# Gated mix of two attentions: how a step's scores and the last output sums are placed at the end of an output block

## The chip, the cores and the metric

The kernel runs on one core of one Trainium2 chip. The metric is the device time of one execution in microseconds (us). A core has TensorE (PE, the matmuls; PEld is its weight load), VectorE (DVE), ScalarE (ACT), GpSimd (POOL) and SyncE (SP, which issues most DMAs). Matmul results land in PSUM, eight banks of 128 x 512 fp32, which TensorE writes and ScalarE and VectorE read.

## The reference

```python
x = A_x                                   # 1 x 2048 x 512
g = sigmoid((x * gate_w).sum(-1, keepdims=True))
# branch A: 32 heads of 16, each position looks at 8 positions, 2 apart, behind it
attn = softmax(where(mask, einsum("bhsd,bhswd->bhsw", q, kg) * scale, -1e9))
a = einsum("bhsw,bhswd->bhsd", attn, vg)... @ wo_A
# branch B: 32 query heads of 16, one key and value head, over all 2048 positions
p = softmax(einsum("bhqd,bkd->bhqk", q, k) * scale)
b = einsum("bhqk,bkd->bhqd", p, v)... @ wo_B
return g * a + (1 - g) * b
```

## The kernel before

**Phases.** A front phase projects queries, keys and values and writes parts of them to DRAM scratch. The main phase (from line 1225) does branch B in 512 steps s = 16 u + kt. A unit u is one block of 512 queries and four heads (32 units), kt is one of 16 blocks of 128 keys. GpSimd works through branch A meanwhile. A short tail writes the last four row blocks of the output.

**One step.** The program is written out in the order in which each engine runs its instructions, by a planner in the kernel itself: `clk` holds its clocks of TensorE, ScalarE and VectorE, and `free` the time at which each PSUM bank comes free, from the constants of line 45. `exp_pair(s, pr)` (line 460) computes the scores of two of the four heads as two matmuls side by side (L465) into a pair of banks, e0 for pr = 0 and e1 for pr = 1 (`eb`), and ScalarE exponentiates the 128 x 1024 scores (L471). `weighted(s)` (line 477) multiplies the four exponentials by the values into the bank `po` (L480). In a usual step the order (line 1243) is `(0, "m2", "m1", 1)`: first scores of s, a pair of maxima in the two banks `m2`, perhaps a single in `m1`, second scores of s, and then `weighted(s - 1)`.

**Maxima.** The exponentials need each row's maximum before its unit begins. It is found by separate score matmuls, "halves" of 128 x 512 (L322), of which there are 2048, with a maximum over each on VectorE: `fill_pair` does two halves side by side in `m2` (tile pm, L344), `fill_one` does one in `m1` (tile ps, L356). `fill_ready(key, slack)` (line 856) gives one out if its bank is free within `slack` of the planner's TensorE clock. `singles(s)` (line 845) spreads over the steps left whatever the pairs, one a step, and the out blocks to come won't cover, so that it is used up by step 488. After that the place of `m2` is used by the tail's first products.

**Out blocks.** At steps 272, 400 and 448, the first of a unit each, `out_phase` (line 768) multiplies four row blocks j of the outputs of both branches by their weights (L780), the last four being left to the tail. The conditions of line 1248 choose the steps. Row x of the four sums in `eb[x % 2]`, so the last one (x = 3) in e1, in 24 items of two matmuls side by side. At item 5 of a row, `turn` (line 641) transposes branch A's part of this row into the other pair of banks (L645), from where ScalarE reads it twice (L651, L652); in the last row that is e0. At the row's end `out_store` (line 674) has ScalarE copy both banks to the tile `two` (L678), GpSimd add the two halves (L681) and SyncE store the sum (L682).

`stream` (line 722) runs the items and fills around them. For the block's length `m2` is given up and its two banks serve as `pd0` and `pd1` for differences: `fill_diff` (line 395) computes a difference of two halves (L393), which ScalarE rectifies (L405), and `fill_sum` (line 413) adds one half to it and takes the maximum of both on VectorE (L417) in `ps` or `po`. These are given out by tests on the planner's clocks in `side_fill` (line 687); `closing` stops new differences in the last items. `weighted(s - 1)` runs in the block's first row. `done` (line 783) is called after each item. Afterwards the banks are `m2` again, and step s goes on with its order.

Of the kernel before, what the change touches and what calls it, by code (L numbers as in the profile page):

```python
# [8 lines left out]
AF = mybir.ActivationFunctionType  # L9
# [32 lines left out]
LEAD, M2S, M1S, MARGIN = 1.5, 0.5, 0.3, 0.12  # L42


T_R, T_LAT, T_EXP, T_RED2, T_RED1, T_W, T_TTR = 0.235, 0.20, 0.92, 1.14, 0.61, 1.21, 0.74
# [3 lines left out]
def gated_mix_kernel(ctx, tc, xt, wa, wk, wq, wo_a, wo_b, out):  # L49
    nc = tc.nc  # L50
# [22 lines left out]
    pp2, m2 = None, None  # L73
# [4 lines left out]
    eb = []  # L78
# [5 lines left out]
    clk = {"pe": 0.0, "act": 0.0, "dve": 0.0}  # L84

    def after(eng, ready, dur):
        clk[eng] = max(clk[eng], ready) + dur
        return clk[eng]
# [188 lines left out]
    def place(v):  # L277
        return v if v <= NB else (v - NB - 1) % (NB - 2)

    def gone(v):  # L280
        return v - NB - 1 if v < 2 * NB - 1 else v - NB + 2
# [16 lines left out]
    free = {"m1": 0.0, "e0": 0.0, "e1": 0.0, "po": 0.0, "d0": 24.0, "d1": 24.0}  # L298
    tasks, shifted = [], set()
    hooks, pool, done = [], 0.0, set()  # L300
# [3 lines left out]
    def mark(inst, end, up=None):  # L304
        marks.append((ups[0] if up is None else up, end, inst.ins.name))

    def fillable():
        return bool(half) or bool(slots) and slots[0][0] < len(stacked) and stacked[slots[0][0]] <= clk["pe"]
# [148 lines left out]

    pe, pexp, exped, homes, turns = [], {}, {}, [], [0]

    def exp_pair(s, pr):  # L460
        bank, key = eb[pr], f"e{pr}"
        u, kt = divmod(s, NJ)
        for odd in range(2):
            b = 64 * odd
            nc.tensor.matmul(bank[:, odd, :], kst[b:b + 64, kt * P:(kt + 1) * P], qst[place(u)][b:b + 64, pr, :], start=True, stop=True)  # L465
        if len(homes) < 6:
            homes.append(px.tile([P, 2, 512], F32, name="pexp", bufs=6))
        k, y = divmod(turns[0] + 1, 2)
        turns[0] += 1
        e = homes[len(homes) - 1 if turns[0] < 6 else (2 * (k % 3) + (y ^ k // 3 % 2) - 1) % 6]  # L470
        got = nc.scalar.activation(e, bank, AF.Exp, scale=SCALE)  # L471
        free[key] = after("act", after("pe", free[key], T_R) + T_LAT, T_EXP)
        mark(got, free[key])
        exped[s] = free[key]
        pexp[s, pr] = e
# [156 lines left out]
    def prepare(j, n):  # L632
        nonlocal pool
        hi, lo = turned[j, 1] = [qst[NB - 2][:, x].rearrange("p (c q) -> p c q", c=C) for x in range(2)]
        own = ob[j // 4][:, :n, j % 4 * P:(j % 4 + 1) * P]
        nc.scalar.activation(hi[:, :n], own, AF.Copy)
        at = after("act", clk["pe"], 0.6)
        nc.gpsimd.tensor_sub(lo[:, :n], own, hi[:, :n].bitcast(F32))
        pool = max(pool, 1e3 * at) + 1300
# [25 lines left out]
    def out_items(j, n):  # L665
        items = []
        for k, m in ((1, n), (0, C)):
            for x, w in ((0, woh), (0, wol), (1, woh)):
                items += [(lambda c=c, x=x, k=k: turned[j, k][x][:, c, :], w[k][:, c, :]) for c in range(m)]
        return items  # L670

    parts, spare = {}, []

    def out_store(j, k):
        nonlocal pool
        del turned[j, 0], turned[j, 1]
        two = p2b[0].tile([P, 2, D], F32, name="two", bufs=2)
        nc.scalar.activation(two, eb[k], AF.Copy)  # L678
        free[f"e{k}"] = after("act", clk["pe"] + T_LAT, 0.92)
        pool = max(pool, 1e3 * clk["act"]) + 1300  # L680
        nc.gpsimd.tensor_add(two[:, 0], two[:, 0], two[:, 1])  # L681
        nc.sync.dma_start(out[0].rearrange("(p j) d -> p j d", j=NJ)[:, j, :], two[:, 0])  # L682

# [84 lines left out]
    def out_phase(js, n, s):  # L768

        m = 3 * (C + n)  # L770
        items = {}

        def mm(b, at):
            x, j, i = at
            if j not in items:
                items[j] = out_items(j, n)
                clk["pe"] = max(clk["pe"], free[f"e{x % 2}"])
            st, mv = items[j][i]
            h = slice(64 * b, 64 * b + 64)
            nc.tensor.matmul(eb[x % 2][:, b, :], st()[h], mv[h], start=(i == 0), stop=(i == m - 1))  # L780
            return T_R

        def done(at):
            x, j, i = at
            if i % 4 == 3:
                run_tasks()
                run_pool()
            if i == (5 if x else 1):
                turn(j, 1 - x % 2)
            if i == (8 if x else 6):  # L790
                later.pop(j)()
            if i == 3 * n and j != js[-1]:
                prepare(js[x + 1], n)
            if i == m - 1:
                out_store(j, x % 2)

        stream([(x, j, i) for x, j in enumerate(js) for i in range(m)], mm, done, s)

# [57 lines left out]
    def fill_ready(key, slack):  # L856
        if fillable() and free[key] <= clk["pe"] + slack:
            clk["pe"] = max(clk["pe"], free[key])
            if key == "m1":
                fill_one()  # L860
            elif half and (not slots or half[0][0] < slots[0][0] or slots[0][0] >= len(stacked)):
                fill_one(m2[:, 0, :], "m2")
            elif slots:
                fill_pair(m2, "m2")
            return True
# [34 lines left out]
    def run_tasks():  # L900
        for task in [t for t in tasks if t[0] <= clk["pe"]]:
            tasks.remove(task)
            task[1](*task[2])
# [113 lines left out]
    def run_pool():  # L1017
        nonlocal pool
        now = clk["pe"] * 1e3
        for h in sorted(hooks, key=lambda h: h[0]):  # L1020
            if h[0] <= now:
                hooks.remove(h)
                h[1](h[2])
                done.add(h[3])
        while pieces and pool < now + 2500:
            if blocked and not blocked[0]():
                break
            blocked.clear()
            x = next(pieces[0], None)
            if x is None:  # L1030
                pieces.clear()
            elif callable(x):
                blocked.append(x)
            else:
                pool = max(pool, now) + x
# [188 lines left out]
        del held[b][1:], read_d[b][1:]  # L1224
    phase2()
    pe.append(tc.alloc_tile_pool(name="weighted", bufs=1, side="right"))
    outs, due = 0, []
    for s in range(NS + 1):
        u, kt = divmod(s, NJ)
        if len(stacked) < NU and s >= 16 * (gone(len(stacked)) + 1):  # L1230
            stack(len(stacked))
        if s < NS and kt == 0 and u not in shifted:
            while u not in shifted:
                clk["pe"] += 0.5
                run_tasks()
                if u not in shifted and left.get(u, 1):
                    assert pause(4)
        v = min(x[0][0] for x in (half, slots, [(NU,)]) if x)
        need = left.get(v, NF // NU)
        steps = 16 * v - 6 - s  # L1240
        short = need - 2.8 * max(0, steps) if v < NU else 0
        lead = (NF - to_go()) / 64 - s / 16
        order = (0, "m2", "m1", 1) if s > 1 else (1, "m2", "m1", 0) if s else ()
        k, n = outs // 4, C - (outs >= NJ - 4)
        if outs == NJ - 4:
            if short > 0 and steps < 2:
                pause(short)
        elif due or outs < NJ and outs // NH in done and kt == 15 and NHG * (k + 1) - 1 in shaped and (lead < LEAD or s >= 16 * (NHG * (k + 2) + 1) - 1):
            if not due:
                prepare(outs, n)  # L1250
                due.append(n)
            else:
                out_phase(list(range(outs, outs + 4)), due.pop(), s)
                outs += 4
        elif short > 0 and steps < 2:
            pause(short)

        for which in order:
            if which == "m2":
                if slots or half:  # L1260
                    fill_ready("m2", M2S)
                else:
                    next(tail, None)
            elif which == "m1":
                if singles(s) and fill_ready("m1", M1S):
                    owing[0] -= 1.0
            elif s < NS:
                exp_pair(s, which)
        if s - 1 in exped:
            weighted(s - 1)  # L1270
            if kt == 0 and s < NS:
                finish_a(u - 1, nc.gpsimd)
        run_tasks()
        run_pool()
# [14 lines left out]
    for x in range(2):  # L1289
        js = slice(2 * x, 2 * x + 2)  # L1290
        two = four[:, x]
# [11 lines left out]
    for k in range(4):  # L1303
        j = NJ - 4 + k
# [48 lines left out]
```

## Time and profile before

| | |
|---|---|
| Time, three runs | 1472.81 us median, 1471.78 to 1473.0 |
| Profiled execution, time | 1471.12 us |
| Profiled execution, span | 1469.1 us |
| Busy share of PE, ACT, DVE, POOL | 99%, 89%, 78%, 65% |
| Granted TensorE clock | full in all 40 slices |

The profile is of one execution. A row of the timeline gives the start in us from the span's start, the duration in us, the engine, the line, the operation, out<-in with its shape and count, and in brackets how long the engine had been idle before and what ended that. A row of the groups gives line, engine, operation and count, then the busy time in us and the mean ns of one, then the idle time before them and who ended it. Busy TensorE is modelled, since matmuls overlap.

### The profile page before, as it was taken

How to read it: one execution, taken by the hardware profiler on the slowest of the kernel's cores; microseconds unless marked ns; L12 is line 12 of the kernel's file. 1: busy time of each engine (PE TensorE's matmuls, PEld its weight loads, DVE VectorE, ACT ScalarE, POOL GpSimd, SP SyncE). 2: the span in 40 equal slices, each digit the busy share in tenths (PEclk: the TensorE clock that was granted, in tenths of full speed). 3: DMA queues.
4: the chain of work that ended last, by engine and by line, in shares of the span. 5: the costliest groups of instructions: out<-in, count | busy, mean ns of one | idle time of the engine just before them, and what ended most of it. 6: DMA issues, size and time to landing. Idle time of an engine off the chain costs nothing.

```text
span 1469.1 us, 29512 instructions
## 1 busy us (share of the span) xinstructions
PE 1454.6 (99%) x10965; PEld 739.7 (50%) x10965; DVE 1141.9 (78%) x1837; ACT 1303.6 (89%) x1706; POOL 951.1 (65%) x1693
## 2 busy tenths in 40 slices
PE   9999999999999999999999999999999999999998
PEld 6899999733333333333333373333333743383334
DVE  6778888788888888788888877888888778778821
ACT  5888988799999999999999989999999889889994
POOL 5731898888988988889888898898851311150000
PEclk9999999999999999999999999999999999999999
DMA  6653342320211210102202111121100000000000
GB/s 225 170 169 113 101 149 68 117 73 25 71 41 49 78 49 31 68 22 69 78 12 71 42 63 46 45 71 41 42 12 12 27 16 2 1 31 1 1 2 29
DMA packets 43912, 85.67 MB, mean 58 GB/s; under 512 B 9520, under 2 KB 25960, under 8 KB 39672
## 3 DMA queue, kind: packets, MB, share of 16 engines
q1 hardware_dynamic: 36632, 44.79, 9.9%
q0 software_dynamic: 6560, 37.95, 7.7%
q8 instruction: 86, 1.41, 0.4%
q10 hardware_dynamic: 576, 1.05, 0.2%
q14 instruction: 58, 0.48, 0.1%
HBM read 57.97 MB, written 25.25 MB: 57 GB/s over the span
## 4 chain that ended last, share of the span: by engine, by line
PE 94%; ACT 2%; POOL 1%; DVE 1%; DMA 1%; issue 1%; SPq 0%; POOLq 0%; ACTq 0%
PE po L480 34%; PE pe L465 25%; PE pf L1082 10%; PE pm L322 8%; PE ps L322 5%; PE pe L780 5%; PE pd L393 3%; PE po L322 1%; ACT pexp L471 1%; PE pf L193 1%; PE pe L1283 1%; DMA ad<-stage 0%; DVE mx L344 0%; DMA xraw<-xt 0%; PE pm L836 0%
## 5 line engine op out<-in xcount | busy, mean ns | idle before, releaser
L471 ACT ACTIVATE pexp<-pe 128x1024 f32<-128x1024 f32 x1024 | 987.8, 1023 | 67.6 <-PE pe L465 63.3
L344 DVE TENSOR_REDUCE mx<-pm 128x2 f32<-128x1024 f32 x475 | 580.1, 1221 | 174.6 <-PE pm L322 172.3
L480 PE MATMUL po<-pexp,vst 128*32 128x512 f32 x4096 | 545.5, 605 | 0.1
L465 PE MATMUL pe<-qst,kst 64*128 64x512 f32 x1984 | 523.3, 459 | 4.6 <-ACT pexp L471 2.5
L465 PEld LDWEIGHTS pe<-qst,kst 64*128 64x128 f32 x1984 | 208.8, 183 | 451.6 <-ACT pexp L471 427.2
L405 ACT ACTIVATE dd<-pd 128x512 f32<-128x512 f32 x367 | 209.0, 604 | 44.7 <-PE pd L393 30.9
L356 DVE TENSOR_REDUCE mx<-ps 128x1 f32<-128x512 f32 x333 | 226.5, 680 | 4.5 <-PE ps L322 1.8
L322 PE MATMUL ps<-kst,qst 62*128 62x512 f32 x503 | 206.5, 410 | 0.1
L322 PE MATMUL pm<-kst,qst 62*128 62x512 f32 x916 | 185.9, 397 | 0.4
L542 POOL TENSOR_TENSOR pr<-aext 128x256 f32<-128x256 f32 x256 | 182.0, 737 | 4.9 <-DMA aext<-ad 4.6
L602 POOL TENSOR_TENSOR oa<-oa,av 128x256 f32<-128x256 f32 x224 | 164.1, 732 | 15.8
L480 PEld LDWEIGHTS po<-pexp,vst 128*32 128x32 f32 x4096 | 80.6, 108 | 170.3 <-issue 161.8
L417 DVE CUSTOM_DVE_ANT_0 dd<-ps,dd 128x512 f32<-128x512 f32 x185 | 127.7, 690 | 34.2 <-PE ps L322 14.2
L417 DVE CUSTOM_DVE_ANT_0 dd<-po,dd 128x512 f32<-128x512 f32 x182 | 125.6, 690 | 29.8 <-PE po L322 12.9
L599 POOL TENSOR_TENSOR av<-aext,lg 128x256 f32<-128x256 f32 x224 | 139.3, 622 | 12.8
L393 PE MATMUL pd<-kd,qst 62*128 62x512 f32 x367 | 143.5, 401 | 2.5 <-ACT dd L405 2.5
L1082 PE MATMUL pf<-wal,xh 64*128 64x384 f32 (+1 forms) x496 | 127.9, 338 | 0.0
L1082 PE MATMUL pf<-wah,xh 64*128 64x384 f32 (+1 forms) x496 | 124.0, 337 | 0.0
L1082 PE MATMUL pf<-wah,xl 64*128 64x384 f32 (+1 forms) x496 | 122.7, 338 | 0.0
L322 PEld LDWEIGHTS ps<-kst,qst 62*128 62x128 f32 x503 | 92.9, 185 | 43.5 <-DVE mx L356 38.6
L506 POOL TENSOR_TENSOR rl<-rl,gate_t 128x16 f32<-128x16 f32 x31 | 6.9, 222 | 157.9 <-DVE rl L500 157.9
L322 PEld LDWEIGHTS pm<-kst,qst 62*128 62x128 f32 x916 | 88.3, 186 | 3.5 <-DVE mx L344 3.0
(199 smaller groups left out, 1725.4 us busy)
## 6 DMA issues: line engine op xcount, KB each, us to landing
aext<-ad POOLq DMA_DIRECT2D x32, 1056.0 KB, 5.4
ad<-stage SPq DMA_DIRECT2D x32, 384.0 KB
qst<-qd SPq DMA_DIRECT2D x62, 128.0 KB
xraw<-xt SPq DMA_DIRECT2D x16, 256.0 KB
qd<-qhi SPq DMA_DIRECT2D x16, 256.0 KB
qd<-qlo SPq DMA_DIRECT2D x16, 256.0 KB
qst<-qd SPq DMA_DIRECT2D x62, 64.0 KB
qst<-ml SPq DMA_DIRECT2D x220, 2.0 KB
```

Of the source, the lines that this page charges most:

```text
L322: nc.tensor.matmul(dst, qst[place(v)][b:b + 62, pr, t * P:(t + 1) * P], kst[b:b + 62, kc * 512:(kc + 1) * 512], start=True, stop=True)
L344: got = nc.vector.tensor_reduce(m[:, :, pr, t, kc], dst, AX.X, ALU.max)
L356: got = nc.vector.tensor_reduce(m[:, odd, pr, t, kc:kc + 1], dst, AX.X, ALU.max)
L393: nc.tensor.matmul(dst, qst[place(v)][b:b + 62, pr, t * P:(t + 1) * P], kd[0][b:b + 62, kc // 2, :], start=True, stop=True)
L405: got = nc.scalar.activation(held[b][k], dst, AF.Relu)
L417: got = nc.vector.tensor_tensor_reduce(held[b][k], dst, held[b][k], 1.0, -FMAX, ALU.add, ALU.max, m[:, b, pr, t, kc:kc + 1])
L465: nc.tensor.matmul(bank[:, odd, :], kst[b:b + 64, kt * P:(kt + 1) * P], qst[place(u)][b:b + 64, pr, :], start=True, stop=True)
L471: got = nc.scalar.activation(e, bank, AF.Exp, scale=SCALE)
L480: nc.tensor.matmul(po[32 * i:32 * i + 32, :], vst[:, kt, :], pexp[s, i // 2][:, i % 2, :], start=(kt == 0), stop=(kt == NJ - 1))
L542: nc.gpsimd.tensor_mul(pr[:, k], q, e[:, o:o + NH, AC:2 * AC])
L602: nc.gpsimd.tensor_add(ao, ao, av)
L1082: inst = nc.tensor.matmul(home(x)[0][:, :n], l[h], r[h], start=(i == 0 and b == 0), stop=(i == 3 * C - 1 and b == 1))
```

## The change

At the end of each out block three things are placed otherwise.

First, in the last row (j the last of the four) from the item after the tenth on, `done` gives out the first scores of step s into e0 as soon as the planner's clock has these banks free, at the latest at the row's last item. Their exp goes into ScalarE's queue at that place.

Second, step s keeps of its order only the second scores, `order = (2,)`, and puts them into the banks `m2` in place of e1. It gives out no pair and no single. In the step after it, the pair in `m2` is granted 1.2 us of the planner's clock to wait for its banks, in place of `M2S` = 0.5.

Third, the last row's sums are copied from e1 to `two` by VectorE in place of ScalarE, planned at 1.15 us. The planner's clock of GpSimd now starts from the copy's end.

```diff
-    def exp_pair(s, pr):
-        bank, key = eb[pr], f"e{pr}"
+    def exp_pair(s, pr, other=False):
+        bank, key = (m2, "m2") if other else (eb[pr], f"e{pr}")
...
-    def out_store(j, k):
+    def out_store(j, k, closing):
...
-        nc.scalar.activation(two, eb[k], AF.Copy)
-        free[f"e{k}"] = after("act", clk["pe"] + T_LAT, 0.92)
-        pool = max(pool, 1e3 * clk["act"]) + 1300
+        if closing:
+            nc.vector.tensor_copy(two, eb[k])
+            free[f"e{k}"] = after("dve", clk["pe"] + T_LAT, 1.15)
+        else:
+            nc.scalar.activation(two, eb[k], AF.Copy)
+            free[f"e{k}"] = after("act", clk["pe"] + T_LAT, 0.92)
+        pool = max(pool, 1e3 * free[f"e{k}"]) + 1300
...
+            if j == js[-1] and i > 9 and s not in exped and (free["e0"] <= clk["pe"] or i == m - 1):
+                exp_pair(s, 0)
             if i == m - 1:
-                out_store(j, x % 2)
+                out_store(j, x % 2, j == js[-1])
...
-    outs, due = 0, []
+    outs, due, led = 0, [], set()
...
+        early = (s - 1, 1) in pexp and s - 1 in led
...
                 out_phase(list(range(outs, outs + 4)), due.pop(), s)
                 outs += 4
+                led.add(s)
+                order = (2,)
...
-                    fill_ready("m2", M2S)
+                    fill_ready("m2", 1.2 if early else M2S)
...
-                exp_pair(s, which)
+                exp_pair(s, which % 2 or which // 2, which == 2)
```

## The prediction, made before the result was known

> **What bounds the kernel now.** I read the page's chain of work first, then the chain in order of time around the three out blocks, then those places' windows, then their timeline.
>
> ```profile
> PE 94%; ACT 2%; POOL 1%; DVE 1%; DMA 1%; issue 1%; SPq 0%; POOLq 0%; ACTq 0%
> ```
>
> ```profile
> 878.50 1.15 PE pe L780 x10
> 882.72 1.02 ACT two L678
> 886.13 1.00 PE po L480 x8
> ```
>
> TensorE carries 94% of the chain; what the change can win is in the few places where the chain leaves it. One is the end of an out block: after the last row's products (L780) the chain runs through ScalarE's copy of their sums (L678), and only some 3 us later through TensorE again. The windows of the first block and of the way from the first scores after each block to the first weighted sum (L480) say how much is at stake:
>
> ```profile
> 848.30:882.50 34.20, 34.20 (x311) 28.73 (x309) 24.66 (x71) 27.98 (x51) 32.21 (x45) 1.00 0.18 61
> 882.50:886.06 3.56, 2.51 (x16) 1.07 (x12) 2.23 (x4) 3.34 (x5) 2.48 (x4) 1.00 0.04 15
> 1180.70:1184.49 3.79, 2.72 (x17) 1.31 (x14) 2.48 (x4) 3.33 (x4) 1.95 (x3) 1.00 0.02 8
> 1313.75:1317.32 3.57, 2.67 (x16) 1.18 (x14) 2.65 (x5) 3.35 (x4) 2.25 (x3) 1.00 0.03 11
> ```
>
> The columns are length, then busy time of PE, PEld, DVE, ACT, POOL. Inside the block TensorE is never idle; in the three short windows ScalarE is busy for 3.3 of 3.6 to 3.8 us, and TensorE idle for about 1 us in each. So the place is bound by a queue on ScalarE. The first block in order of time, where s is the block's step (the first of its unit):
>
> ```profile
> 882.50 0.42 PE L465 MATMUL pe<-qst,kst 64*128 64x512 f32 x2
> 882.72 1.02 ACT L678 ACTIVATE two<-pe 128x1024 f32<-128x1024 f32 x1 [1.04 <-PE pe L780]
> 882.72 0.43 PE L322 MATMUL pm<-kst,qst 62*128 62x512 f32 x2
> 883.64 1.94 ACT L471 ACTIVATE pexp<-pe 128x1024 f32<-128x1024 f32 x2
> 883.80 0.51 PE L465 MATMUL pe<-qst,kst 64*128 64x512 f32 x2 [0.64 <-ACT two L678]
> 884.71 0.50 PE L465 MATMUL pe<-qst,kst 64*128 64x512 f32 x2 [0.41 <-ACT pexp L471]
> 885.05 0.39 PE L322 MATMUL pm<-kst,qst 62*128 62x512 f32 x2
> 885.28 0.39 PE L322 MATMUL ps<-kst,qst 62*128 62x512 f32 x1
> 885.63 0.50 PE L465 MATMUL pe<-qst,kst 64*128 64x512 f32 x2
> 886.06 1.06 PE L480 MATMUL po<-pexp,vst 128*32 128x512 f32 x8
> ```
>
> The rows are: first scores of s (882.50), a pair of maxima (pm), second scores of s (883.80, which waited for the copy of their banks e1), first scores of s+1 (884.71, which waited for the exp of s in banks e0), a pair, a single (ps), second scores of s+1, weighted sum of s. Seven issues 0.23 apart and 0.43 from the last one to the weighted sum would need 6 x 0.23 + 0.43 = 1.81 us; the chain took 3.56. Some 1.7 us is waiting. The other blocks take as long, 1184.49 - 1180.81 = 3.68 and 1317.32 - 1313.75 = 3.57:
>
> ```profile
> 1180.81 0.54 PE L465 MATMUL pe<-qst,kst 64*128 64x512 f32 x2
> 1184.49 1.06 PE L480 MATMUL po<-pexp,vst 128*32 128x512 f32 x8
> ```
>
> ```profile
> 1313.75 0.57 PE L465 MATMUL pe<-qst,kst 64*128 64x512 f32 x2
> 1317.32 1.07 PE L480 MATMUL po<-pexp,vst 128*32 128x512 f32 x8
> ```
>
> **First scores into the last row.** The two matmuls of 0.23 us are moved, not added. Their exp (1.02 us, between 883.64 and the 884.66 after which 884.71 starts) moves too, into ScalarE's queue among the last row's differences (L405). Is there room?
>
> ```profile
> 877.96 0.64 ACT L652 ACTIVATE qst<-pe 128x512 fp32r<-128x512 f32 x1
> 880.59 1.09 ACT L405 ACTIVATE dd<-pd 128x512 f32<-128x512 f32 x2 [1.01 <-PE pd L393]
> ```
>
> ```profile
> 1178.90 1.22 ACT L405 ACTIVATE dd<-pd 128x512 f32<-128x512 f32 x2 [0.95 <-PE pd L393]
> 1311.62 1.09 ACT L405 ACTIVATE dd<-pd 128x512 f32<-128x512 f32 x2 [1.02 <-PE pd L393]
> ```
>
> Banks e0 hold the turned row until the second reader (L652) ends, 878.60 in the first block. The plan gives the scores out at the first item past the tenth at which its clock has e0 free. By the constants in the code that is 0.5 + 0.2 + 1.3 = 2.0 us or a little more after the turn at item 5. At 0.24 us an item and more with the side work, that is item 12 to 14 of 24, about 3 us before the row's end (882.7), so near 879.5. ScalarE stands idle for 1.01, 0.95 and 1.02 us ahead of the last two differences of the three blocks. An exp of 1.02 fits there almost exactly, if the scores come as early as reckoned. I take no delay; the other end is that the exp starts just ahead of the differences and pushes them back by 1.02, and TensorE, which has their sums (L417) behind them in its own order, by as much: 0 to 3 x 1.02 = 3.06 us. Nothing below zero: no instruction leaves the row.
>
> **Second scores in m2, copy on VectorE.** The scores of s no longer wait for e1. On the clock that is 0 at 882.50 in the first block: with the first scores now inside the row, the second go out at 0.23, and the first of s+1 at 0.46 (e0 has long been read). From scores to exp takes:
>
> ```profile
> 889.18 0.50 PE L465 MATMUL pe<-qst,kst 64*128 64x512 f32 x2
> 889.73 1.94 ACT L471 ACTIVATE pexp<-pe 128x1024 f32<-128x1024 f32 x2 [0.19 <-PE pe L465]
> ```
>
> that is 0.55, so the exp runs from 0.78 to 1.80. Here is the wait that the change adds: step s+1 first fills m2 with a pair of maxima, and these banks are now under that exp. Step s+1 grants 1.2 us of the plan's clock for it (`early`), where it granted 0.5. Behind this pair in TensorE's order stand the single, the second scores of s+1 and the weighted sum of s. TensorE stands from 0.69 to 1.85 (0.05 after the exp, as at 884.71). Then pair 1.85, single 2.08, second scores 2.31, weighted sum 2.31 + 0.43 = 2.74.
>
> The second scores of s+1 write e1, which VectorE must have copied by 2.31:
>
> ```profile
> 882.24 0.69 DVE L417 CUSTOM_DVE_ANT_0 dd<-ps,dd 128x512 f32<-128x512 f32 x1
> 1180.80 0.69 DVE L417 CUSTOM_DVE_ANT_0 dd<-po,dd 128x512 f32<-128x512 f32 x1 [0.16 <-PE po L322]
> 1313.94 0.69 DVE L356 TENSOR_REDUCE mx<-po 128x1 f32<-128x512 f32 x1
> ```
>
> ```profile
> L344 DVE TENSOR_REDUCE mx<-pm 128x2 f32<-128x1024 f32 x475 | 580.1, 1221 | 174.6 <-PE pm L322 172.3
> L678 ACT ACTIVATE two<-pe 128x1024 f32<-128x1024 f32 x12 | 12.3, 1027 | 3.7 <-PE pe L780 3.4 <-PE pd L393 0.2
> L1319 DVE COPY osl<-ps 128x256 f32<-128x256 f32 x1 | 0.4, 424 | 6.3 <-ACT osl L1318 6.3
> ```
>
> No VectorE copy of 128x1024 is in the trace. The nearest is the reduction that reads as much from PSUM, 1.22 us; the ends are 1.03 (ScalarE's copy) and 4 x 0.424 = 1.70 (four copies of a quarter). I take 1.22, since the quarter's 424 ns holds the fixed part of every instruction. VectorE's last work of the row ends at 0.51, 0.76 (the first two with 0.08 for reading the sum out) and 0.88, so the copy ends at 1.73, 1.98 and 2.10. That is ahead of 2.31 by 0.2 us at the least; at 1.70 the third would be 0.27 late. VectorE's next work is the pair at 1.85, whose maxima are due back only a step later. GpSimd's addition and SyncE's store (L681, L682) follow the copy and move by under 1 us; nothing waits for them soon.
>
> [...]
>
> So the gain to the weighted sum is 3.56 - 2.74 = 0.82, 3.68 - 2.74 = 0.94 and 3.57 - 2.74 = 0.83, together **2.59 us**.
>
> **What is given back.** Step s now gives out no pair of maxima (its order is `(2,)`): three pairs, six halves. Every later step already has its one pair in m2, so `singles` spreads the six over later steps as lone matmuls. What one costs:
>
> ```profile
> 1205.23 1.07 PE L480 MATMUL po<-pexp,vst 128*32 128x512 f32 x8
> 1206.81 0.45 PE L322 MATMUL ps<-kst,qst 62*128 62x512 f32 x1
> 1207.41 1.06 PE L480 MATMUL po<-pexp,vst 128*32 128x512 f32 x8
> 1209.30 1.07 PE L480 MATMUL po<-pexp,vst 128*32 128x512 f32 x8
> ```
>
> The step with a single takes 2.18 us, the next without one 1.89: 0.29. Its place in the order is 0.23 (885.28 - 885.05). I take 0.23, six times 1.38 us; the other end is 0, if such steps had slack on TensorE. No further halves are lost: the row's differences are given out by the same tests, where the exp puts ScalarE's planned end back by 0.92 and the tests grant 0.7 to 2.2.
>
> **Sum.** -2.59 + 1.38 = -1.21 us. The profiled execution took 1471.12 (span 1469.1 and 2.0 around it), 1.69 below the median 1472.81. It would take 1469.9, and the median **1471.6**, 0.08% less.
>
> **Rivals.** (a) *ScalarE's queue in the row, slower.* The exp comes too late for its gap and pushes the differences, so the row waits instead of the steps. Against it: gaps of 0.95 to 1.02 us, and another idle 1.04 (at 882.72) behind them; for it: the gap fits to within 0.07 us. At 1.02 per block: 1471.6 + 3.06 = 1474.7. It decides once the row grows by over 1.21 / 3 = 0.40 us per block. Chance 0.2. (b) *The lost halves cost nothing*, as ScalarE's two exps (1.94 us together) set a step's pace: 1472.81 - 2.59 = 1470.2. Against it: the step of 1.89 above. Chance 0.17. (c) *It doesn't do what it says*: the plan has e0 free only at the row's last item. Then the first scores go out where they do now (0), both exps run after the row, from 0.55 to 1.57 and to 2.59, the pair follows at 2.64 and the weighted sum at 2.64 + 0.23 + 0.23 + 0.43 = 3.53. The gain shrinks to 0.03 + 0.15 + 0.04 = 0.2 us and 1.38 is still given back: 1474.0. Against it: 2.0 us from item 5 on end long before item 24. Chance 0.08. The forecast has 0.55.
>
> **Numbers.** About 0.2% (2.9 us) is what a measurement of this kernel tells from no change. The forecast and (c) lie within it; (b) with its spread reaches past 1469.9 about half the time, and some of the forecast's own upper gain does; (a) with lost differences on top passes 1475.7 in under half its cases. Faster 0.14, within 0.77, slower 0.09. The range takes in (b) with a little of the run's spread (1.2 us) and (a): 1469.8 to 1474.6.
>
> **What would show it.** Right: an exp (L471) ahead of the last differences in each block, a VectorE copy of 1.2 us at L678's place, weighted sum 2.7 us after the old place of the first scores, a wait of a little over 1 us before the pair of step s+1, six more singles (ps) over the later steps. Wrong: longer blocks (the first one's 34.2 us), second scores of s+1 waiting for the copy, or blocks at other steps, since the plan decides by its clock.

## The result and the profile after

| | before | changed |
|---|---|---|
| Median, range | 1472.82 us, 1470.65 to 1475.12 (20 executions) | 1469.94 us, 1468.71 to 1471.32 (20 executions) |
| Ratio | | 0.9981, 95% interval 0.9975 to 0.9987 |
| Profiled execution, time | 1471.12 us | 1470.24 us |
| Profiled execution, span | 1469.1 us | 1468.4 us |

The changed kernel is 2.8 us faster (1.9 to 3.7), more than twice the 1.21 us of the forecast, 0.14 us inside the end of its range, and with 0.19% just short of the 0.2% that the forecast called faster. The shares of the chain of work, from the page of the changed kernel:

```profile
PE 95%; ACT 1%; POOL 1%; DVE 1%; issue 0%; DMA 0%; SPq 0%; POOLq 0%; ACTq 0%
```

ScalarE's share went from 2% to 1%, TensorE's from 94% to 95%. These are whole per cents of 1468 us, some 15 us each, so they can't show a change of a few us; the rows of the timeline can. The timeline of the changed kernel at the end of the first block:

```profile
880.65 0.45 PE L465 MATMUL pe<-qst,kst 64*128 64x512 f32 x2
881.17 1.03 ACT L471 ACTIVATE pexp<-pe 128x1024 f32<-128x1024 f32 x1
882.24 1.09 ACT L405 ACTIVATE dd<-pd 128x512 f32<-128x512 f32 x2
...
884.14 0.45 PE L465 MATMUL pm<-qst,kst 64*128 64x512 f32 x2
884.38 0.45 PE L465 MATMUL pe<-qst,kst 64*128 64x512 f32 x2
884.74 1.22 DVE L679 COPY two<-pe 128x1024 f32<-128x1024 f32 x1
884.98 1.02 ACT L471 ACTIVATE pexp<-pm 128x1024 f32<-128x1024 f32 x1 [1.65 <-PE pe L465]
886.06 0.50 PE L322 MATMUL pm<-kst,qst 62*128 62x512 f32 x2 [1.23 <-ACT pexp L471]
...
886.96 1.07 PE L480 MATMUL po<-pexp,vst 128*32 128x512 f32 x8
887.04 1.23 DVE L344 TENSOR_REDUCE mx<-pm 128x2 f32<-128x1024 f32 x1 [1.08 <-PE pe L465]
```

Most of it is as the prediction drew it. The first scores (880.65) and their exp (881.17) stand in the row, and the exp ends at 882.20, just ahead of the last two differences (882.24). The second scores (884.14) go into `m2`, and the first ones of s+1 follow at 0.24. VectorE's copy takes 1.22 us. TensorE waits 1.23 us for the exp of the second scores before the pair of s+1 (886.06), and the weighted sum of s starts 0.90 after it.

The third block, from the timeline of the kernel before (start of the block, last transposition of the turn, weighted sum of s+1; that of s started at 1317.32, a row that the prediction shows):

```profile
1281.19 0.73 PE L780 MATMUL pe<-woh,qst 64*128 64x512 f32 x4
1308.14 0.22 PE L645 MATMUL pe<-ident,oa 64*128 64x64 f32 x1
1319.46 0.64 PE L480 MATMUL po<-pexp,vst 128*32 128x512 f32 x4
```

and from that of the changed kernel, with the weighted sums of s and of s+1:

```profile
1281.52 0.50 PE L784 MATMUL pe<-woh,qst 64*128 64x512 f32 x2
1308.83 0.22 PE L645 MATMUL pe<-ident,oa 64*128 64x64 f32 x1
1317.10 1.07 PE L480 MATMUL po<-pexp,vst 128*32 128x512 f32 x8
1319.37 1.06 PE L480 MATMUL po<-pexp,vst 128*32 128x512 f32 x8
```

So the rows up to the turn take 1308.83 - 1281.52 = 27.31 us instead of 26.95, from the turn to the weighted sum of s 8.27 instead of 9.18, the next step 2.27 instead of 2.14. The start of the last transposition is a good mark: it lies ahead of everything that the change moves. Read in the same way, all three blocks and what lies between (us; "again" is a second profile of the kernel before, "no grant" an experiment below):

| stretch | before | before, again | changed | no grant |
|---|---|---|---|---|
| block 1: rows to the turn | 27.50 | 27.46 | 27.47 | 27.43 |
| turn to weighted sum of s | 9.01 | 9.01 | 8.46 | 7.95 |
| step s+1 | 2.13 | 2.12 | 2.62 | 2.13 |
| steps to block 2 | 260.67 | 260.63 | 260.51 | 260.64 |
| block 2: rows to the turn | 26.70 | 26.71 | 26.75 | 26.64 |
| turn to weighted sum of s | 8.93 | 8.92 | 7.84 | 7.79 |
| step s+1 | 2.13 | 3.71 | 2.12 | 2.14 |
| steps to block 3 | 94.57 | 94.55 | 94.72 | 95.11 |
| block 3: rows to the turn | 26.95 | 26.97 | 27.31 | 27.67 |
| turn to weighted sum of s | 9.18 | 9.17 | 8.27 | 7.47 |
| step s+1 | 2.14 | 2.13 | 2.27 | 2.13 |
| steps to the last weighted sum | 125.87 | 125.82 | 125.43 | 127.20 |
| all | 595.78 | 597.20 | 593.77 | 594.30 |

From the first block's start to the last weighted sum the changed kernel is 2.01 us shorter than the first profile of before. Between turn and weighted sum it wins 0.55 + 1.09 + 0.91 = 2.55, in the step after that it loses 0.49 + 0.13 - 0.01 = 0.61, in the rows 0.36 + 0.05 - 0.03 = 0.38, and the steps behind the blocks are 0.16 + 0.44 - 0.15 = 0.45 shorter. The second profile of before holds another 1.58 us, all in one step behind block 2; that is taken up below.

What became of the lost halves is read from the groups. The page of the kernel before:

```profile
L405 ACT ACTIVATE dd<-pd 128x512 f32<-128x512 f32 x367 | 209.0, 604 | 44.7 <-PE pd L393 30.9
L322 PE MATMUL ps<-kst,qst 62*128 62x512 f32 x503 | 206.5, 410 | 0.1
L322 PE MATMUL pm<-kst,qst 62*128 62x512 f32 x916 | 185.9, 397 | 0.4
L393 PE MATMUL pd<-kd,qst 62*128 62x512 f32 x367 | 143.5, 401 | 2.5 <-ACT dd L405 2.5
```

and of the changed kernel:

```profile
L405 ACT ACTIVATE dd<-pd 128x512 f32<-128x512 f32 x373 | 212.2, 604 | 42.0 <-PE pd L393 28.3
L322 PE MATMUL ps<-kst,qst 62*128 62x512 f32 x503 | 207.2, 412 | 0.1
L322 PE MATMUL pm<-kst,qst 62*128 62x512 f32 x910 | 184.4, 398 | 3.3 <-ACT pexp L471 3.1
L393 PE MATMUL pd<-kd,qst 62*128 62x512 f32 x373 | 146.6, 403 | 2.3 <-ACT dd L405 2.2
```

There are six matmuls less in `m2` (pm, 916 to 910) and six differences more (pd, 367 to 373). The tile ps, which holds the steps' singles and some of the blocks' lone halves, has 503 in both; counted by their place in the traces, 140 of them stand outside the blocks in both kernels, so no single was added. A difference lets a lone half of a block take the maximum of two, so the halves came back inside the blocks, not as singles over the steps. Two of the added differences stand at block 2 and four in block 3's rows. Up to their turn these rows now hold 55 matmuls for maxima instead of 49, and they are the rows that grew by 0.36; from the turn to the block's end there are 9 instead of 11. The last stretch, 0.44 shorter, has 23 singles instead of 25.

### The profile page after: what moved, and what is told of

Its sections match the earlier page's. It is cut to its first block, busy times and chain, and to the rows that moved or that the text cites. A ratio compares the mean times of both kernels' runs of the same rounds, so it can differ in the third digit from the quotient of the medians.

```text
span 1468.4 us, 29511 instructions
## 1 busy us (share of the span) xinstructions
PE 1455.3 (99%) x10965; PEld 743.0 (51%) x10965; DVE 1142.1 (78%) x1842; ACT 1304.2 (89%) x1709; POOL 951.1 (65%) x1693
## 4 chain that ended last, share of the span: by engine, by line
PE 95%; ACT 1%; POOL 1%; DVE 1%; issue 0%; DMA 0%; SPq 0%; POOLq 0%; ACTq 0%
PE po L480 34%; PE pe L465 25%; PE pf L1088 10%; PE pm L322 8%; PE ps L322 5%; PE pe L784 5%; PE pd L393 3%; PE po L322 1%; PE pf L193 1%; ACT pexp L471 1%; PE pe L1292 1%; DMA ad<-stage 0%; DVE mx L344 0%; PE pm L842 0%; PE ps L1292 0%
## 5 line engine op out<-in xcount | busy, mean ns | idle before, releaser
L344 DVE TENSOR_REDUCE mx<-pm 128x2 f32<-128x1024 f32 x473 | 577.7, 1221 | 172.4 <-PE pm L322 169.2
L465 PE MATMUL pe<-qst,kst 64*128 64x512 f32 x1978 | 522.8, 459 | 1.6 <-ACT pexp L471 1.3
L465 PEld LDWEIGHTS pe<-qst,kst 64*128 64x128 f32 x1978 | 209.1, 184 | 445.3 <-ACT pexp L471 423.3
L405 ACT ACTIVATE dd<-pd 128x512 f32<-128x512 f32 x373 | 212.2, 604 | 42.0 <-PE pd L393 28.3
L393 PE MATMUL pd<-kd,qst 62*128 62x512 f32 x373 | 146.6, 403 | 2.3 <-ACT dd L405 2.2
```

The source lines that it names most:

```text
L344: got = nc.vector.tensor_reduce(m[:, :, pr, t, kc], dst, AX.X, ALU.max)
L393: nc.tensor.matmul(dst, qst[place(v)][b:b + 62, pr, t * P:(t + 1) * P], kd[0][b:b + 62, kc // 2, :], start=True, stop=True)
L405: got = nc.scalar.activation(held[b][k], dst, AF.Relu)
```

## The experiments

Ratios are to the kernel before on the same chip, with their 95% intervals. Two theories run through them. W: the waits are what counts, and lost halves cost nothing that can be measured. G: the waits saved and 0.23 us given back for each half, as forecast.

**One part alone: the pair dropped.** The kernel before without the pair of step s (a block's step gives out no single in either kernel, since `singles` says no at the first step of a unit):

```diff
                 outs += 4
+                order = (0, 1)
```

> The kernel before, but the three block steps give out no pair of maxima; scores, exps and copy stay where they are. Only the lost halves are tried. Theory G (my prediction: the six halves come back as six single matmuls at 0.23 us each): 1472.8 + 1.4 = 1474.2. Theory W (the gain is all in the waits; the blocks take the halves up as differences and six single maxima in the blocks become differences): 1472.8, within 0.4.

Measured: 1472.95 us, ratio 1.0003 (0.9994 to 1.0012), so +0.4 us, nearer to W; the interval's end of 1.8 doesn't exclude G's 1.38. What settles the matter is the groups of this kernel:

```profile
L322 PE MATMUL ps<-kst,qst 62*128 62x512 f32 x503 | 206.7, 411 | 0.0
L322 PE MATMUL pm<-kst,qst 62*128 62x512 f32 x910 | 184.6, 397 | 0.3
L393 PE MATMUL pd<-kd,qst 62*128 62x512 f32 x373 | 145.6, 402 | 2.2 <-ACT dd L405 2.2
```

The same exchange as in the changed kernel: the lost halves become differences, whatever else the change does. Two of them stand at block 2 and four at block 3 here too, and these blocks' rows take 26.80 and 27.02 us, only 0.10 and 0.07 more than in the kernel before.

**One part alone: the copy on VectorE.**

```diff
+        if closing:
+            nc.vector.tensor_copy(two, eb[k])
+            free[f"e{k}"] = after("dve", clk["pe"] + T_LAT, 1.15)
+        else:
...
-                out_store(j, x % 2)
+                out_store(j, x % 2, j == js[-1])
```

> The kernel before, with only the last row's copy moved to VectorE. Both theories: the exp of the first scores starts 0.6 us earlier, but the second scores wait in e1 for the copy to about 1.8 to 2.1 us, where ScalarE had it done at 1.2, so that the weighted sum comes some 0.3 us later per block: 1473.7. It also loses seven halves of maxima outside the blocks, which Theory G prices at 1.6 us more: 1475.3.

Measured: 1475.85 us, ratio 1.0019 (1.0009 to 1.0029): slower by 2.8 us. The second scores still go to e1 here, so the slower copy is what they wait for:

```profile
885.46 0.73 PE L465 MATMUL pe<-qst,kst 64*128 64x512 f32 x4 [0.97 <-DVE two L679]
```

Turn to weighted sum took 9.15, 9.43 and 9.98 us, 1.44 more than before in all. The number is G's (2.5 us more; W's 0.9 lies outside the interval of 1.3 to 4.3), and there are five matmuls more in ps (508). But the profiled execution (mean clock 0.995) also had its clock halved in the front phase and behind blocks 2 and 3, which neither theory holds, so the number alone doesn't decide between them. Without the second scores in the other banks the copy on VectorE loses.

**One part undone: the copy back on ScalarE.** The changed kernel with `out_store(j, x % 2, False)`.

> The changed kernel, with the last row's copy back on ScalarE: copy from about 0.45 to 1.42, exp of the second scores to 2.42, weighted sum at about 3.3 in place of 2.7, so a gain of only 0.2 to 0.3 us per block is left. It loses 13 halves of pairs. Theory W: about 1472.1. Theory G: 13 x 0.23 = 3.0 us on top, 1475.1.

Measured: 1470.27 us, ratio 0.9985 (0.9976 to 0.9994). Both theories missed: nothing was lost. The planner, with another clock of ScalarE, left out the pair of step s+1 too, so TensorE had no wait for its banks (turn to weighted sum 7.92, 7.81, 7.51). So this kernel differs in two things from the changed one; "no grant" below separates them.

**One part alone: the first scores in the row.**

```diff
+            if j == js[-1] and i > 9 and s not in exped and (free["e0"] <= clk["pe"] or i == m - 1):
+                exp_pair(s, 0)
...
+                order = ("m2", 1)
```

> The kernel before, with only the first scores of the block step given out in the last row; second scores in e1 as before, copy on ScalarE, and no pair lost. Both theories: the second scores still wait for the copy, their exp ends near 3.0 and the weighted sum follows at 3.5, as before: 1472.6, within 0.5. If the row itself were lengthened by the exp in ScalarE's queue (the prediction's slower rival), up to 1 us per block more: 1475.7.

Measured: 1471.11 us, ratio 0.9990 (0.9981 to 0.9999). Turn to weighted sum is nearly as before, 9.04, 9.01 and 9.00, as expected: the copy still holds e1. That it is 1.5 us faster all the same was not expected. In its profile, as in the first of before, the step behind block 2 takes 2.14 us, at full clock. And its way from the first block to the last weighted sum takes 594.85 us, 0.93 less than before, 0.55 of it in the last stretch (125.33), where 22 singles stand instead of 25. So a planner that deals out the side work otherwise is worth up to 1 us here, without any wait removed.

**Keep TensorE busy.** I then had a theory on the clock, C: waits of TensorE behind a block halve its granted clock in some executions. Three pairs of matmuls without a use, which nobody reads, were put into the first wait of the kernel before (in `m2`), and three single ones into the wait of the changed kernel (in `m1`):

```diff
+                order = (0, "busy", "m2", "m1", 1)
...
+            elif which == "busy":
+                for _ in range(3):
...
+                        nc.tensor.matmul(m2[:, odd, :], kst[h, kt * P:(kt + 1) * P], qst[place(u)][h, 0, :], start=True, stop=True)
```

> The kernel before, with three pairs of extra matmuls (their results are overwritten unread) after the first scores of each block step, where TensorE waits for ScalarE's copy anyway: 0.69 us of work in a wait of 0.85. Nothing else moves. Theory W (the waits alone make the difference between the two kernels, 2.5 us): 1472.7, within 0.4. Theory C (some executions of the kernel before also lose granted clock after the block, as the run without the pair did at 1184 us, because TensorE does too little there): about 0.9 us less, 1471.8, and a narrower spread.

> The changed kernel, with three extra matmuls of 0.22 us (results overwritten unread) in the 1.2 us in which step s+1 waits for its pair. Theory W: 1469.9, within 0.4, since they lie inside the wait. Theory C, if this wait too costs clock in some executions: up to 0.9 us less, 1469.0.

Measured: 1471.96 us (1470.85 to 1472.54), ratio 0.9999 (0.9990 to 1.0008), and 1469.72 us, ratio 0.9982 (0.9973 to 0.9990). The first spread less than the kernel before beside it (1.7 us in 11 executions against 3.6 in 26) and has no halved clock at the blocks in its profile, but isn't faster; the second is as the changed kernel. C isn't borne out by these two. Nor is it excluded: the first one's interval, 1.5 us less to 1.2 more, takes in C's 0.9 less, and the added matmuls lengthened its way from the first block to the last weighted sum by 0.35 us (596.13).

**Further in the same direction.** The changed kernel with the second scores in the row too, in the banks of two differences, with an exp for each bank; step s then has nothing left to give out:

```diff
+            if j == js[-1] and i > m - 6 and (s, 0) in pexp and (s, 1) not in pexp and (i == m - 1 or max(stream_at[-1]) > len(js) * m - 6 and max(free["d0"], free["d1"]) <= clk["pe"]):
+                exp_split(s)
...
-                order = (2,)
+                order = ()
```

> The changed kernel, with the second scores of the block step given out before the row's last items too, into the two banks of the differences, with two exps of 128x512 in place of one of 128x1024. Their exp starts some 0.7 us earlier, so the pair's wait shrinks from 1.2 to about 0.5 us and VectorE's copy becomes what the weighted sum waits for, at 2.4 in place of 2.7. Theory W: 0.35 us per block less, 1468.9; it also gives five more single maxima outside the blocks and four halves fewer in pairs, which at 0.23 us each would take 1.2 us back: 1470.0 if singles cost what the prediction took.

> The kernel with the second scores given out in the row too, again, beside the changed kernel on the same chip. If its lead is real: 0.6 to 0.9 us below the changed kernel (1469.0), ratio to the kernel before 0.9977. If not: within 0.3 of it.

Measured: 1469.04 us, ratio 0.9977 (0.9968 to 0.9986), which is W's number, and again 1469.21 us, ratio 0.9977 (0.9968 to 0.9986). It beats both kernels: over all its 21 executions the mean is 1469.22, over the changed kernel's 31 it is 1469.80, 0.58 less, with a scatter of 0.64 and 0.71 us (so 2 x sqrt(0.64² / 21 + 0.71² / 31) = 0.38 of uncertainty). At the end of its first block TensorE's wait before the pair is down from 1.23 to 0.71 us:

```profile
883.14 1.08 ACT L486 ACTIVATE pexp<-pd 128x512 f32<-128x512 f32 x2 [1.07 <-PE pd L484]
884.28 0.50 PE L322 MATMUL pm<-kst,qst 62*128 62x512 f32 x2 [0.71 <-ACT pexp L486]
```

That this is what makes it faster isn't shown. Its two profiles take 593.64 and 593.79 us from the first block to the last weighted sum, the changed kernel's 593.77 and 593.80, since block 3's rows (27.66 and 27.69 to the turn) and the last stretch (126.12 and 126.17, with 26 singles) take back what the waits give. Behind its second block the wait is one for the copy (L693 here), which is what would have to be moved next:

```profile
1182.37 0.49 PE L465 MATMUL pe<-qst,kst 64*128 64x512 f32 x2 [1.10 <-DVE two L693]
```

**The price of a single.** The changed kernel with the pair of s+1 granted no longer wait than elsewhere, so that it is left out:

```diff
-                    fill_ready("m2", 1.2 if early else M2S)
+                    fill_ready("m2", M2S)
```

> The changed kernel with the pair of step s+1 granted 0.5 us of the plan's clock as elsewhere, so that the planner leaves this pair out and TensorE doesn't wait for the exp of the second scores (1.23, 0.95 and 0.94 us in the changed kernel's profile). Its halves come back as singles (the program has 951 halves in pairs and 333 singles, the changed one 958 and 325). A (TensorE's time is the bound there, a single costs 0.23 us): 3.1 us of waits less, some 8 singles more, -3.1 + 8 x 0.23 = -1.3, so 1468.6. B (ScalarE's two exps a step are the bound just behind the block; what TensorE doesn't wait for the pair it waits for them, or pays in the later steps): within 0.4 of the changed kernel's 1469.9.

Measured: 1469.66 us, ratio 0.9980 (0.9971 to 0.9989), beside the changed kernel's 1469.89 on that chip: B's number. The table above tells why: TensorE doesn't wait for ScalarE instead, it pays in the later rows and steps. Turn to weighted sum and the step after it are shorter by 1.00, 0.03 and 0.94, 1.97 us in all; 0.36 of it is lost in block 3's rows; and then the last stretch takes 127.20 instead of 125.43. There stand the added singles. The stretch from 1317 to 1400, counting only the singles' tile ps, in the changed kernel:

```profile
1317.00:1400.00 83.00, 9.68 (x23) 4.26 (x23) 16.33 (x24) 0.00 (x0) 1.00 0.01 4
```

and in this one:

```profile
1317.00:1400.00 83.00, 12.29 (x29) 5.34 (x29) 19.75 (x29) 0.00 (x0) 1.00 0.02 5
```

The first count is that of the matmuls: six more. (127.20 - 125.43) / 6 = 0.30 us for each single, if all of it is theirs (the stretch also has one pair less): the price that the prediction read from a step with and a step without one (0.29), a little above the 0.23 that it took. Kernels whose last stretch differs in its singles alone give less: 22 singles and 125.33 us with the first scores alone, 25 and 125.88 in the kernel before, 26 and 126.12 with the second scores in the row, so 0.18 and 0.24 each. So a single does cost TensorE time, 0.2 to 0.3 us, and rival (b)'s reason is wrong; the change was spared it only because its halves did not become singles. This kernel beside the one with the copy on ScalarE also shows what the copy's place is worth without that pair: next to nothing up to the weighted sum (7.95, 7.79, 7.47 against 7.92, 7.81, 7.51), but with the copy on ScalarE the step after it takes 2.46, 2.26 and 2.27 instead of 2.13 or 2.14, and the whole way from the first block to the last weighted sum 595.01 us instead of 594.30.

**The clock.** The kernel before twice more, and the changed one once more, to sort times by the mean granted clock of each execution:

> The kernel before, once more, for its profile. Theory W: full granted clock at the ends of the three blocks, as in the first profile. Theory C: in some profiles of it the clock drops there.

> The changed kernel again, for its times by granted clock. P (path 2.0 us, the rest is the clock): executions at the full mean clock (1.000) come out 1.7 to 2.0 us below those of the kernel before at the same clock, and the kernel before has more executions at 0.998 or less. Q (all path): 2.8 us at the same clock. By the runs so far: the changed kernel 1468.96 at 1.000 (6 executions), the kernel before 1470.55 to 1470.74 (3 and 4 executions).

> The kernel before again, for its times by granted clock, beside the changed kernel on the same chip. Ratio to itself 1.000 +- 0.001; P and Q as said for the changed kernel's run: P has it at 1470.7 at clock 1.000, Q at 1471.7.

Measured: 1472.89 us in the single profiled execution, then 1469.89 us (ratio 0.9980, 0.9971 to 0.9989) and 1472.46 us (ratio 1.0000, 0.9991 to 1.0008). All executions whose clock was listed, 101 of the kernel before and 31 of the changed one, sorted by their mean granted clock:

| mean clock | before: executions, median | changed: executions, median | apart |
|---|---|---|---|
| 1.000 | 10, 1470.74 us | 10, 1469.01 us | 1.73 |
| 0.999 | 58, 1472.27 us | 11, 1469.97 us | 2.30 |
| 0.998 | 24, 1473.46 us | 10, 1470.48 us | 2.98 |
| 0.997, 0.996 | 9, 1473.77 us | none | |

At full clock they are 1.73 apart, as P said. P's other half did not come: at 0.998 or less there are 33% of the executions of before and 32% of the changed ones, and at 0.998 the two lie further apart than Q's 2.8. So equal means don't stand for equal losses, and it counts where the clock is lost. The mean also counts a halved end of the span, where no matmul is left (the last 1.5 us in the changed kernel's profile): the two profiles of the changed kernel have the same single loss before that, but means of 0.998 and 0.999. The path is worth some 1.7 to 2.0 us of the 2.8.

The traces show where the rest may come from. By the windows of five profiles (the front phase in the changed kernel's two and in that of the copy alone on VectorE, behind block 2 in the second and third of before) a halved stretch lasts 3.40 to 3.41 us. Both profiles of the changed kernel have one such stretch in the front phase and none behind a block. The second and third profiles of the kernel before have one behind block 2 and none in the front phase. With the front one the first block starts about 1 us later: at 850.35 to 851.03 in the eight profiles, of all kernels, that have it, and at 849.40 to 850.01 in the six that don't. The one behind block 2 costs 1.58, as the windows of the second profile show. This fits the medians, which rise by 0.96 from 1.000 to 0.999 in the changed kernel and by 1.53 in the kernel before. The windows go from the first scores behind block 2 on; the column before the last two is the granted clock:

```profile
1181.00:1184.80 3.80, 2.72 (x17) 1.33 (x14) 2.49 (x4) 3.32 (x4) 1.96 (x3) 1.00 0.02 5
1184.80:1188.50 3.70, 3.70 (x17) 1.32 (x15) 1.94 (x3) 2.39 (x3) 0.00 (x0) 0.54 0.19 66
```

against the same place in the first profile of before:

```profile
1181.00:1184.50 3.50, 2.43 (x16) 1.02 (x12) 2.29 (x4) 3.34 (x4) 1.95 (x3) 1.00 0.03 11
1184.50:1188.00 3.50, 3.50 (x29) 1.32 (x27) 2.99 (x4) 3.28 (x4) 0.00 (x0) 1.00 0.19 65
```

The same program with the same waits ahead of it (8.92 and 8.93 from turn to weighted sum) does 17 matmuls at half clock in one execution where it does 29 at full clock in another, and step s+1 takes 3.71 us instead of 2.13.

## Why the prediction was right, and where it was wrong

**What bounds the place: right.** ScalarE's queue behind the block held TensorE, and taking two pieces out of it shortened the way from turn to weighted sum by 0.55, 1.09 and 0.91 us.

**First scores into the row at no cost: right.** They went out at the time reckoned, 880.65 with the turn at 878.50, and their exp (881.17 to 882.20) fits the gap ahead of the last differences. So it does in the other two blocks, where these differences start at 1180.53 and 1312.39:

```profile
1179.60 1.03 ACT L471 ACTIVATE pexp<-pe 128x1024 f32<-128x1024 f32 x1 [0.38 <-PE pe L465]
1311.46 1.03 ACT L471 ACTIVATE pexp<-pe 128x1024 f32<-128x1024 f32 x1 [0.24 <-PE pe L465]
```

Rival (a), that the exp pushes them back, would show as a longer way from the turn to the second scores of s. That takes 5.64, 5.48 and 5.39 us; in the kernel before it is 5.45, 5.25 and 5.61 to the first scores, to which 0.23 must be added for their issue. No block is longer. Rival (c), e0 free only at the row's end, did not come about.

**The waits, 2.59 us: right in the sum, partly by luck in the parts.** Measured are 2.55, but as 0.55, 1.09 and 0.91 where 0.82, 0.94 and 0.83 were forecast. From the second scores to the weighted sum the prediction had 2.74 - 0.23 = 2.51; it took 2.82, 2.36 and 2.88. The exp of the second scores started 0.84, 0.62 and 0.92 after them and not 0.55: in block 1 the profile puts its start down to the first scores of s+1, and in block 3 the second of the two matmuls itself started 0.43 after the first. What made up for it was not foreseen: block 2's step s+1 has no single, and in block 3 there is less side work between the turn and the second scores. What the prediction did not follow is the step behind it: in block 1, 0.49 of the gain was lost at once. VectorE began the pair's maxima only at 887.04, 0.48 after the matmuls at 886.06 had run, and the single's and the next pair's maxima are queued behind them. The changed kernel's weight loads of step s+2 show TensorE waiting for these:

```profile
888.32 0.19 PEld L322 LDWEIGHTS pm<-kst,qst 62*128 62x128 f32 x2 [0.18 <-DVE mx L344]
888.91 0.18 PEld L322 LDWEIGHTS ps<-kst,qst 62*128 62x128 f32 x1 [0.41 <-DVE mx L356]
```

It wasn't the copy: that ended at 885.96, and VectorE then stood idle for 1.08 us. The profile puts the delay down to the second scores of s+1 (L465), which come after the pair on TensorE; in block 3 the same reduction started 0.12 after its pair. The changed kernel's second profile has the delay again, with 2.63 us for the step. Why block 1 differs is not settled.

**The copy at 1.22 us: right**, to the last digit, three of three:

```profile
L679 DVE COPY two<-pe 128x1024 f32<-128x1024 f32 x3 | 3.7, 1220 | 0.0
```

The forecast put four quarters (1.70) aside for their fixed part. As an estimate from the maxima of the kernel before (680 ns for 128 x 512, 1221 for 128 x 1024) that part is 2 x 680 - 1221 = 139 ns.

**What is given back, 1.38 us: wrong, and this is the step that failed.** "`singles` spreads the six over later steps as lone matmuls" did not happen: the singles outside the blocks stayed at 140, differences rose by six. Not the price was off (0.2 to 0.3 measured for a single that is added) but the count, which was 0 instead of 6. In its place 0.38 us were given back in the rows (0.14 with the pair dropped alone). Why the planner takes differences here is not settled; the pair dropped alone does the same, so it isn't the moved exp or the copy.

**The sum.** Of the path, -2.55 + 0.61 + 0.38 - 0.45 = -2.01 us in the profiles and -1.73 at equal clock; forecast -1.21. The 0.45 at the end, which the forecast had at nothing, fits the two singles less in the last stretch, which is 0.44 shorter. Rival (b)'s 1470.2 lies near the measured median of 1469.94, but for a reason that the runs contradict. The remaining 0.8 to 1.1 us of the 2.8 come with the granted clock, which the prediction, made from one profile with full clock throughout, could not see. That the change removes the halved clock behind block 2 is likely but not shown as a cause. No profile of a kernel with the first scores in the row has it at a block's end, and four of the six others do; but the kernel with the first scores alone waits as long as before and has none, filling the wait gained nothing, and the changed kernel was profiled only twice.

## What to carry to other kernels

When work is dropped from a place, find in the program where it comes back, and count it there: six halves cost 0.2 to 0.3 us each as lone matmuls, and 0.36 / 6 = 0.06 as six more matmuls in a block's rows. A wait that is removed is worth what the next two steps keep of it (here 2.55 became 1.94 after one), so follow each engine's queue a step past the point where the wait ended. And where a forecast is about a few us in a thousand, one profile is a thin base: here it had full clock throughout, which only 10 of 101 executions have.

## What was not expected of the hardware

In these profiles TensorE's granted clock falls to half for 3.41 us at places where it had been partly idle, in some executions and not in others. In the front phase, in common code, the changed kernel's profile has it,

```profile
215.00:216.00 1.00, 0.00 (x0) 0.00 (x0) 0.31 (x2) 0.64 (x2) 0.87 (x3) 1.00 0.99 331
218.00:219.00 1.00, 1.00 (x9) 1.00 (x8) 0.42 (x3) 1.00 (x4) 1.00 (x2) 0.50 0.00 0
```

and the first profile of the kernel before, idle there for longer (TensorE for 2.23 us without a break, the changed kernel for 1.93), does not:

```profile
215.00:216.00 1.00, 0.00 (x0) 0.00 (x0) 0.21 (x2) 0.43 (x2) 0.92 (x3) 1.00 0.94 315
218.00:219.00 1.00, 1.00 (x14) 1.00 (x12) 0.86 (x3) 1.00 (x4) 1.00 (x2) 1.00 0.00 0
```

In the first the matmuls of that microsecond are 9 instead of 14. The changed kernel's clock records hold full clock for 211.63 us from the first record on (6.05 us into the span), half for 3.413, and full again for 1245.87; those of the first profile of before hold full clock for 1464.32 us from 4.22 on, up to a halved end. To within 0.15 us these three lengths are 62, 365 and 429 times 3.413. So, as an estimate from these two profiles, the clock changes only at steps of this length, counted from the first record. Laid out in them, one step of the changed kernel's profile holds most of the front pause (214.26 to 217.67, TensorE busy for 1.48 of 3.41 us, then the drop), while in the first profile of before an edge at 215.85 divides the pause (1.92 and 2.66 us busy, no drop). But busy time alone doesn't decide: in the second profile of before TensorE was busy for 2.33 of the 3.41 us ahead of the drop behind block 2 (it waited for 0.66 and 0.42), and 2.18 us in a step at the end of the changed kernel's first block (883.27 to 886.68) brought no drop.
